# An mLSTM cell followed by a squared-ReLU FFN: k and q pairs a chunk earlier, squares ahead of the numerators' round trip, one marker ahead of a rounding step

## The chip, the cores and the metric

The kernel runs on one core of a Trainium2 chip. The metric is the device time of one execution in microseconds. Three runs of the kernel before took 496.23, 498.50 and 497.52 us; the median is 497.52.

The engines are named as in the profile: PE is TensorE (PEld its weight loads), DVE is VectorE, ACT is ScalarE, POOL is GpSimd, SP is SyncE. DMAs are issued by SP ("SPq") and by POOL, each in the order of its program, and so an issue that waits holds up those behind it.

## What is computed

The first half is an mLSTM cell over 4 batches, 8 heads, 768 steps and a head width of 40:

```
m_new = max(f + m, i);  f_stab = exp(f + m - m_new);  i_stab = exp(i - m_new)
C = f_stab*C + i_stab * outer(v, k);   n = f_stab*n + i_stab*k
y = sigmoid(o) * (C q) / max(|n q|, 1)
```

The second half takes the 3072 rows of 8 x 40 = 320 values as tokens and computes `square(max(x @ w_in, 0)) @ w_out` with w_in of 320 x 2048 and w_out of 2048 x 320.

## The kernel before, in words

**Chunks.** The recurrence is cut into chunks of 128 steps: s = 0 to 23, six to a batch (c = s mod 6 is the place in the batch). Inside a chunk it becomes attention: scores k.q (PE), weights from the gates (ACT), their product (`weighted`, L552, DVE), and matmuls with the values and with the carried state C into the numerators `numT`. Two chunks (256 tokens, a group g) feed one group of the FFN.

**Order.** The order of the program is written out by hand; nothing is scheduled by costs. From chunk 6 on, one loop over `parts` takes n = 0, 1, 2, ...: s = 6 + n // 4 is the chunk, at = n % 4 its quarter, and each part has a quarter of an FFN stage for PE to run beside the attention. From chunk 8 on, even chunks hold the FFN's second product (`ffn2_fast`, L890, a seven-product scheme) and odd chunks the first (`ffn1_open`, `ffn1_close`, L966 and L1015).

**Transposing through DRAM.** k and q are needed with the head width on partitions. `pair_up(s)` copies k and q of chunk s from the inputs to a DRAM tensor `kq_rows`, in pairs of heads, with four DMAs (L308; by SP for s < 10, else by POOL). `load_squares(s)` reads it back as blocks of 32 x 32 with four DMAs on SP (L363) into one of two buffers `kqT` (s mod 2). `turn_kq(s)` transposes the blocks on DVE (L370). Then `scores(s)` can run (L530), and `scale_q` multiplies q by the decays (L600). In even chunk s, quarter 0 has scores(s), turn_kq(s + 1) and weighted(s); scores(s + 1) follow in quarter 1.

**Attention and the marker.** `attend_begin(s)` issues the first half of the numerators' matmuls (L636, L655, L666) and then the marker, a DVE instruction on one element (L628) that reads the result and writes a spare element of an operand of the second half; so the second half (`attend_end`) starts only after the first is through. After that DVE transposes the numerators into `tn` (L686).

**The numerators' round trip.** `store_num` writes tn to DRAM (L701, SP) and `load_num` reads it back with four DMAs (L706), which turns it the rest of the way. `normalise_turned(s)` (L718 to L731, DVE, quarter 2) divides by the denominator and multiplies by the output gate. The rows x make a like round trip: `store_rows` (L757), `load_rows` into xT (L762), `turn_squares` (L769). `load_A` (L394) brings the cumulated decays, which POOL masks (L431) and ACT exponentiates (L461); POOL also forms values times weights (vw, L481) and sums of x for the FFN (L958). Finished tokens go out with L926 and L931 in even chunks.

**Rounding of the weights.** The FFN weights come as pairs of 32-bit words and are put together in 18 pieces: two ACT steps (`words`), three DVE steps (L222, L226, L227) and an addition on POOL (L231). The last piece, two blocks of w_out, is rounded in part n = 4, the first of chunk 7. In part n = 5 the buffers of the rounding are given back (`brought.close()`) and the pool `late` is opened over them; DVE first writes there with L864.

**SP's order in chunk s >= 8, as far as the change touches it:** quarter 1: store_num(s), load_num(s), load_squares(s + 2); then load_A(s + 2) (in even chunks here), the stores of tokens, x rows, the output gate, xT. The squares have to wait for their pairs in `kq_rows`, and for the last reader of their buffer.

Of the kernel before, what the change touches and what calls it, by code (L numbers as in the profile page):

```python
# [14 lines left out]
ALU = mybir.AluOpType  # L15
# [5 lines left out]
def word_as_float(w):  # L21
    return struct.unpack("<f", struct.pack("<I", w))[0]
# [7 lines left out]
def kernel(  # L30
# [27 lines left out]
    nc = tc.nc  # L58
# [33 lines left out]
    brought = ExitStack()  # L92
# [81 lines left out]
    class Rounding:  # L174
# [38 lines left out]
            nc.scalar.activation(low[:, :w], raw[:, :, 0].bitcast(U32), AF.Copy, bias=2.0, scale=2.0 ** -51)  # L213
            self.a.append((mag, low))

        def join(self):
            n = len(self.b)
            dst = pieces[n][0]
            w = dst.shape[1]
            mag, low = (t[:, :w] for t in self.a[n])  # L220
            bits = mag.bitcast(I32)
            nc.vector.tensor_scalar(  # L222
                mag, mag, scalar1=word_as_float(0x38000000), scalar2=word_as_float(0x47EFFFFF),
                op0=ALU.max, op1=ALU.min,
            )
            nc.vector.tensor_scalar(bits, bits, scalar1=3, scalar2=None, op0=ALU.logical_shift_left)  # L226
            nc.vector.scalar_tensor_tensor(  # L227
                bits, in0=self.raws[n][:, :w, 1], scalar=-0x80000000, in1=bits,
                op0=ALU.bitwise_and, op1=ALU.bitwise_xor,
            )  # L230
            nc.gpsimd.tensor_tensor(dst.bitcast(I32), bits, low.bitcast(I32), op=ALU.add)  # L231
            self.b.append(None)
            if n != LENT - 1:
                self.fetch()

        @property
        def done(self):
# [9 lines left out]
    rounding = Rounding()  # L247
# [261 lines left out]
    def scores(s, o=(False, False)):  # L509
        d = st[s]  # L510

        sc = [bank(o[i]) for i in range(2)]
        d["sc"] = sc
        if s >= KQ_SQ:
            if s >= ROT:
                d["sc"] = [t.rearrange("p j t -> p (j t)")[:, : 3 * P].rearrange("p (e t) -> p e t", e=2) for t in sc]
            for e in range(2):
                for late_keys in range(2):
                    for c in range(2):
                        for i in range(2):  # L520
                            rows = slice(DP * i, DP * i + D)
                            start = e == late_keys == 0
                            if s < ROT:
                                j, keys = 2 * late_keys + e, HALVES[c]
                                to, t0 = sc[i][HALVES[c], j, :], 0
                            else:
                                j, keys = 2 * (c ^ late_keys) + e, HALVES[late_keys]
                                to = d["sc"][i][HALVES[c], e, slice(0, DP) if late_keys else slice(DP, 3 * DP)]
                                t0 = DP * late_keys
                            nc.tensor.matmul(  # L530
                                to, lhsT=d["kT"][rows, j, keys], rhs=d["qT"][rows, j, t0:], start=start, stop=True,
                                skip_group_check=True,
                            )
            return
        for j in range(PR):
            for i in range(2):
                rows = slice(DP * i, DP * i + D)
                nc.tensor.matmul(  # L538
                    sc[i][:, j, :], lhsT=d["kT"][rows, j, :], rhs=d["qT"][rows, j, :], start=True, stop=True,
                )  # L540
# [462 lines left out]
    def ffn1_rows(g, q, first):  # L1003
        xT, xs = st["xT", g], st["xs"]
        X, Y, V, Z = st["f1"]
        lo, hi = HALVES
        pairs = (
            ((X, lo, xT[lo, 0, 2, :], False), (Y, hi, xT[hi, 1, 2, :], first)),
            ((V, lo, xT[lo, 1, 2, :], first), (Z, hi, xs[hi, 1, :], False)),
        )  # L1010
        for pair in pairs:
            for n in range(4):
                for cols in HALVES:
                    for to, rows, rhs, start in pair:
                        nc.tensor.matmul(  # L1015
                            to[cols, n, :], lhsT=w_in2[rows, 4 * q + n, cols], rhs=rhs,
                            start=(start and n == 0), stop=True, skip_group_check=True,
                        )
# [35 lines left out]
    def do(f, s):  # L1054
        if 0 <= s < NT:
            f(s)
# [86 lines left out]
    for u in range(8):  # L1143
        s = 2 + u // 2
# [72 lines left out]
    LAST = (17, 17, 17, 17, 18)  # L1217
    assert LAST[-1] == len(pieces)

    for n, (which, g, i) in enumerate(parts):  # L1220
        s, at = 6 + n // 4, n % 4
        if n == 5:
            brought.close()
            late = ctx.enter_context(tc.tile_pool(name="late", bufs=1, side="right"))
        even = s >= 8 and s % 2 == 0
        fast = which == 1
        if at == 0:
            if s < 8 or even:
                do(scores, s)
            if even:  # L1230
                do(turn_kq, s + 1)
            if s < 8 or even:
                do(weighted, s)
        if at == 1:
            do(attend_begin, s)
            if even:
                do(lambda s: scores(s, ("h", "h")), s + 1)
            if fast:
                ffn1_rows(g, 0, True)
            do(attend_end, s)  # L1240
            do(decays, s + 1)
            do(mask, s + 1)
            if n > 4 and not even and not fast:
                do(turn_kq, s + 1)
            do(decay_C, s + 1)
            if s > X_SQ and not fast and not even:
                do(turn_squares, s - 1)
            do(store_num, s)
            do(load_num, s)
            do(load_squares, s + 2)  # L1250
            if even:
                do(load_A, s + 2)
        if 5 <= n < 8:
            sums_of_weights(n - 5)
        if n == 6:
            sums(1, slice(0, NPAIR), (1, 2))
        if n == 8:
            sums_of_weights(3)
            sums(1, slice(0, NPAIR), (3,))
        if n == 9:  # L1260
            sums(1, slice(0, NPAIR), (4,))
        if which == 2 and i == 3 and g == NG - 2:
            sums(g + 1, slice(0, NPAIR), (2,))
        if which == 2 and g > 1 and i < 2:
            sums(g, slice(0, NPAIR), (3 + i,))
        if n == 0:
            ffn1_begin(g)
            sums_of_x(g)
            sums_of_win(2)
        if at == 3 and s >= 8 and s % 2 == 0 and s // 2 - 1 < NG:  # L1270
            sums_of_x(s // 2 - 1)
        if at == 2 and not fast:
            if even:
                do(turn_squares, s - 1)
            if n > 4:
                do(scale_q, s + 1)
        if at == 3:
            if s % 4 == 3:
                for r in range(s + 1, min(s + 5, NT)):
                    half_tanh(r)  # L1280
        if fast:
            if i % 2:
                ffn1_close(g, i // 2, i == 1)
                if at == 1 and g > 2:
                    do(turn_kq, s + 1)
                    do(turn_squares, s - 1)
            else:
                ffn1_open(g, i // 2)
                if i == 0 and g > 2:
                    sums(g - 1, slice(0, NPAIR), (2,))  # L1290
            if at == 2 and g > 2:
                do(scale_q, s + 1)
        elif g == 0:
            ffn2(g, *divmod(i, 2))
        else:
            ffn2_fast(g, i)
        if at == 2:
            do(lambda s: weigh(s, masked=True), s + 1)
            ffn1_square()
            if n < 4:  # L1300
                do(turn_kq, s + 1)
                do(scale_q, s + 1)
            if even:
                do(weighted, s + 1)
            do(normalise_turned, s)
            do(store_rows, s)
            if not even:
                do(load_A, s + 2)
            if s > 6:
                do(load_o, s + 5)  # L1310
            do(load_rows, s)
            if s == 6:
                do(pair_up, s + 3)
        if s > 6 and at == (3 if even else 2):
            do(pair_up, s + 3)
        if s > 6 and at == 3:
            if s == 7:
                load(s + 3)
            do(load, s + 4)
        if n == 3:  # L1320
            turn_halves()
        if n in (9, 25):
            spread_slots(2 + n // 25)
        if at == 0:
            ffn1_square()
        if n < 5:
            while rounding.done < LAST[n]:
                rounding.step()


# [28 lines left out]
```

## Time and profile before

| | us |
|---|---|
| median of three runs | 497.52 |
| the profiled execution | 497.72 |
| its span | 496.0 |
| PE busy | 486.8 |
| PE weight loads busy | 452.8 |
| DVE busy | 346.6 |
| ACT busy | 241.6 |
| POOL busy | 224.6 |

The span is the time from the first instruction of the program to the last; the rest of an execution lies around it. The matmuls' ends are modelled, so that a busy PE can hide short waits; stages that do the same work are therefore compared by their length. Lines such as L370 are lines of the kernel before. In a timeline, a row has its start and its duration in us, the engine, line and operation, what it writes and reads, how many instructions, and in brackets the idle time of the engine before it and who ended that.

### The profile page before, as it was taken

The page shows a single profiled execution, that of the slowest core. Times are in us where ns is not written, and L with a number is a line of the kernel's source. Part 1 is how long each engine was busy: PE and PEld are TensorE (multiplying, and loading weights), DVE is VectorE, ACT ScalarE, POOL GpSimd, SP SyncE. Part 2 cuts the span into 40 slices and gives each one's busy share as a digit, 9 for nine tenths or more (in the row PEclk, how much of TensorE's full clock was granted, in tenths as well). Part 3 has the DMA queues.
Part 4 walks back from the last instruction along what each step waited for, and adds up shares of the span by engine and source line. Part 5 has one row for each costly group of instructions (what it writes and reads, how often), then busy time and mean ns, then how long its engine had stood idle before and what let it go on. Part 6 is the DMA issues. An engine that isn't in the chain of part 4 may idle for free.

```text
span 496.0 us, 15226 instructions
## 1 busy us (share of the span) xinstructions
PE 486.8 (98%) x6169; PEld 452.8 (91%) x6169; DVE 346.6 (70%) x700; ACT 241.6 (49%) x530; POOL 224.6 (45%) x317
## 2 busy tenths in 40 slices
PE   9999989999999999999999999999999999999997
PEld 4877878897799999999999989999999999999997
DVE  8599968978956866866956856766856956735441
ACT  3658878756531560761562850561861560423300
POOL 3256734532589438558547538538544030020000
PEclk9999999999999999999999999999999999999999
DMA  9999996757698678678668768677666532200000
GB/s 189 226 215 213 276 210 143 207 90 138 150 151 187 136 140 177 142 136 178 148 128 177 158 119 170 148 139 166 149 126 142 121 69 80 54 15 15 3 26 28
DMA packets 196167, 68.02 MB, mean 137 GB/s; under 512 B 158704, under 2 KB 186064, under 8 KB 196096
## 3 DMA queue, kind: packets, MB, share of 16 engines
q1 hardware_dynamic: 190560, 57.50, 56.6%
q0 software_dynamic: 5440, 9.34, 8.2%
q8 instruction: 49, 0.80, 0.7%
q14 instruction: 22, 0.18, 0.1%
q10 hardware_dynamic: 96, 0.20, 0.1%
HBM read 54.71 MB, written 18.01 MB: 147 GB/s over the span
## 4 chain that ended last, share of the span: by engine, by line
PE 84%; DVE 10%; DMA 2%; issue 1%; SPq 1%; POOL 0%; DVEq 0%; POOLq 0%
PE h_ps L890 34%; PE h_ps L966 23%; PE h_ps L1015 6%; PE h_ps L799 3%; PE h_ps L836 3%; PE numT L655 2%; PE numT L636 2%; DVE mag L226 2%; PE hp L575 1%; PE idle L1065 1%; PE numT L666 1%; PE tp L538 1%; DMA kqT<-kq_rows 1%; DVE mag L227 1%; PE tp L530 1%
## 5 line engine op out<-in xcount | busy, mean ns | idle before, releaser
L890 PE MATMUL h_ps<-T,S 128*128 128x160 f32 x352 | 51.7, 300 | 0.0
L996 ACT COPY r_sb<-h_ps 128x512 f32<-128x512 f32 x18 | 10.6, 586 | 84.2 <-PE h_ps L966 84.2
L890 PEld LDWEIGHTS h_ps<-T,S 128*128 128x128 f32 x352 | 48.9, 190 | 0.4 <-ACT g_c L1032 0.2
L890 PE MATMUL h_ps<-w_out,g 128*128 128x160 f32 x336 | 49.2, 303 | 0.0
L906 DVE TENSOR_TENSOR y_sb<-y_sb,h_ps 128x160 f32<-128x160 f32 x44 | 14.1, 320 | 47.6 <-PE h_ps L890 47.6
L890 PEld LDWEIGHTS h_ps<-w_out,g 128*128 128x128 f32 x336 | 46.1, 190 | 1.3 <-issue 0.7
L431 POOL TENSOR_SCALAR_AFFINE_SELECT A_bc<-A_bc 64x512 f32<-64x512 f32 x32 | 23.2, 726 | 43.5 <-ACT kq L448 42.2
L966 PE MATMUL h_ps<-xT,w_in 128*128 128x128 f32 x320 | 42.8, 278 | 0.0
L966 PE MATMUL h_ps<-lent_t,w_in 128*128 128x128 f32 x320 | 42.2, 275 | 0.0
L966 PEld LDWEIGHTS h_ps<-xT,w_in 128*128 128x128 f32 x320 | 38.9, 192 | 1.4 <-issue 1.0
L1015 PE MATMUL h_ps<-xT,w_in 64*64 64x128 f32 x960 | 39.1, 272 | 0.0
L966 PEld LDWEIGHTS h_ps<-lent_t,w_in 128*128 128x128 f32 x320 | 38.9, 192 | 0.2 <-issue 0.2
L966 PE MATMUL h_ps<-lent_t 128*128 128x128 f32 x320 | 39.0, 275 | 0.0
L966 PEld LDWEIGHTS h_ps<-lent_t 128*128 128x128 f32 x320 | 37.3, 192 | 0.0
L1015 PEld LDWEIGHTS h_ps<-xT,w_in 64*64 64x64 f32 x960 | 34.8, 133 | 1.3
L461 ACT ACTIVATE A_bc<-A_bc,b_R 128x64 f32<-128x64 f32 (+1 forms) x128 | 35.7, 361 | 0.4
L340 POOL DMA_DIRECT2D va<-in_v_dram x56 | 34.4, 620 | 1.7 <-DMA va<-in_v_dram 0.9
L481 POOL TENSOR_TENSOR vw<-va,A_bc 128x328 f32<-128x328 f32 x13 | 10.2, 788 | 52.3 <-ACT A_bc L461 52.3
L686 DVE STREAM_TRANSPOSE tn<-numT 128x256 f32<-128x256 f32 x36 | 14.0, 429 | 28.4 <-PE numT L636 19.6
L958 POOL TENSOR_TENSOR lent_t<-xT 128x128 f32<-128x128 f32 (+1 forms) x18 | 13.4, 764 | 38.5 <-DVE xT L769 35.5
L799 PE MATMUL h_ps<-xT,w_in 128*128 128x256 f32 x128 | 29.6, 383 | 0.7 <-POOL w_in L231 0.7
L890 PE MATMUL h_ps<-w_out,g_c 128*128 128x160 f32 x192 | 28.0, 302 | 0.0
(200 smaller groups left out, 1189.5 us busy)
## 6 DMA issues: line engine op xcount, KB each, us to landing
A_bc<-a_slots SPq DMA_DIRECT2D x32, 256.0 KB, 4.9
num_rows<-tn SPq DMA_DIRECT2D x18, 256.0 KB, 2.3
kq<-num_rows SPq DMA_DIRECT2D x72, 64.0 KB, 2.0
raw<-in_moe_w_out_dram SPq DMA_DIRECT2D x7, 640.0 KB, 5.3
kqT<-kq_rows SPq DMA_DIRECT2D x34, 128.0 KB, 3.0
og<-in_o_gate_dram SPq DMA_DIRECT2D x24, 160.0 KB, 5.3
out_dram<-y_sb SPq DMA_DIRECT2D x24, 160.0 KB, 3.2
raw<-in_moe_w_in_dram SPq DMA_DIRECT2D x7, 512.0 KB, 5.8
```

The costliest lines, as they stand in the source:

```text
L340: eng.dma_start(dst[HALVES[n], PR * (1 - late_keys) : PR * (2 - late_keys)], src[HALVES[late_keys], PR * m : PR * (m + 1)],)
L431: nc.gpsimd.affine_select(part, part, compare_op=ALU.is_ge, fill=-1e30, base=0, pattern=[[0, PR], [0, 2], [1, DP]], channel_multiplier=-1,)
L461: nc.scalar.activation(A[0][:, x, to], A[0][:, x, to], AF.Exp, bias=b_R[:, b, c, own, x : x + 1],)
L686: nc.vector.transpose(to[:, 2 * m : 2 * m + 2], d["numT"][m].rearrange("p c t -> p (c t)"))
L799: nc.tensor.matmul(hs[i][:, n, :], lhsT=w_in[:, a, fb * P : (fb + 1) * P], rhs=xT[:, :, a, :], start=(n == 0 and a == 0), stop=False,)
L836: nc.tensor.matmul(o_ps, lhsT=st["g2", g][:, fb, j * P : (j + 1) * P], rhs=w_out[:, fb, :], start=(fb == 0), stop=(fb == NF - 1),)
L890: nc.tensor.matmul(to, lhsT=lhsT[:, p], rhs=rhs[:, p, :], start=(start and p == 0), stop=(p == NPAIR - 1), skip_group_check=True,)
L906: add = lambda to, a, b: nc.vector.tensor_tensor(to, a, b, op=ALU.add)
L958: sub = lambda to, a, b: eng.tensor_tensor(to, a, b, op=ALU.subtract)
L966: nc.tensor.matmul(to[:, n, :], lhsT=lhsT[:, 4 * q + n, :], rhs=rhs, start=(start and n == 0), stop=True, skip_group_check=True,)
L996: nc.scalar.copy(m1[:], X[:])
L1015: nc.tensor.matmul(to[cols, n, :], lhsT=w_in2[rows, 4 * q + n, cols], rhs=rhs, start=(start and n == 0), stop=True, skip_group_check=True,)
```

## The change

Three things move; no arithmetic and no DMA is added or removed.

1. `pair_up` runs one chunk earlier: in chunk s it now takes s + 4 instead of s + 3. Chunk 7 does both 10 and 11.
2. From chunk 8 on, `load_squares` no longer follows `load_num`. Even chunk s issues the squares of s + 2 in quarter 0, ahead of its store_num, and those of s + 3 at the end of quarter 3, after the token store L931 and ahead of store_num of chunk s + 1. Odd chunks issue none.
3. The last rounding step's DVE work is split: the first two instructions (L222, L226) stay in part n = 4, the third (L227) comes after the marker of chunk 7, in part n = 5, followed by POOL's addition. The pool `late` is opened after that instead of at the start of the part.

```diff
-        def join(self):
+        def join(self, till=None):
...
-            nc.vector.tensor_scalar(
-                mag, mag, scalar1=word_as_float(0x38000000), scalar2=word_as_float(0x47EFFFFF),
-                op0=ALU.max, op1=ALU.min,
-            )
-            nc.vector.tensor_scalar(bits, bits, scalar1=3, scalar2=None, op0=ALU.logical_shift_left)
+            if till == 1:
+                self.join_to(mag, bits)
+                return
+            if till is None:
+                self.join_to(mag, bits)
             nc.vector.scalar_tensor_tensor(
                 bits, in0=self.raws[n][:, :w, 1], scalar=-0x80000000, in1=bits,
                 op0=ALU.bitwise_and, op1=ALU.bitwise_xor,
...
+        def join_to(self, mag, bits):
+            nc.vector.tensor_scalar(
+                mag, mag, scalar1=word_as_float(0x38000000), scalar2=word_as_float(0x47EFFFFF),
+                op0=ALU.max, op1=ALU.min,
+            )
+            nc.vector.tensor_scalar(bits, bits, scalar1=3, scalar2=None, op0=ALU.logical_shift_left)
...
-        if n == 5:
-            brought.close()
-            late = ctx.enter_context(tc.tile_pool(name="late", bufs=1, side="right"))
...
             if s < 8 or even:
                 do(weighted, s)
+            if even:
+                do(load_squares, s + 2)
         if at == 1:
             do(attend_begin, s)
+            if n == 5:
+                rounding.join(2)
...
             do(store_num, s)
             do(load_num, s)
-            do(load_squares, s + 2)
+            if s < 8:
+                do(load_squares, s + 2)
             if even:
                 do(load_A, s + 2)
+        if n == 5:
+            brought.close()
+            late = ctx.enter_context(tc.tile_pool(name="late", bufs=1, side="right"))
...
         if s > 6 and at == (3 if even else 2):
-            do(pair_up, s + 3)
+            if s == 7:
+                pair_up(s + 3)
+            do(pair_up, s + 4)
...
+        if even and at == 3:
+            do(load_squares, s + 3)
...
         if n < 5:
-            while rounding.done < LAST[n]:
+            while rounding.done < LAST[n] - (n == 4):
                 rounding.step()
+            if n == 4:
+                while len(rounding.a) < LAST[n]:
+                    rounding.words()
+                rounding.join(1)
```

## The prediction, made before the result was known

> **What bounds the kernel now.** I read the page first: TensorE is busy nearly throughout, and the chain that ended last runs mostly over it.
>
> ```profile
> PE 486.8 (98%) x6169; PEld 452.8 (91%) x6169; DVE 346.6 (70%) x700; ACT 241.6 (49%) x530; POOL 224.6 (45%) x317
> PE 84%; DVE 10%; DMA 2%; issue 1%; SPq 1%; POOL 0%; DVEq 0%; POOLq 0%
> ```
>
> The change adds and removes no arithmetic, so it can only win or lose gaps of TensorE after about 120 us. To find these I went through the chain in order of time and compared equal stages. From the first L890 block of an even chunk to its second block (step 0 of the FFN product, then the attention) takes 6.95 us in chunks 8, 10, 14 and 22, but 8.74 us in chunk 16 (282.44 to 291.18). Chunks 12 and 18 start a batch and have fewer matmuls: 6.57 and 7.12 us. Odd chunks repeat to 0.02 us (29.82 us, or 29.36 where the batch ends). So what this part of the kernel loses is 1.79 us in chunk 16, 0.55 in chunk 18, about 0.2 each in 12 and 20. The waits of VectorE tell why in two lines:
>
> ```profile
> DVE dm L718 <- DMA kq<-num_rows: 4.2, 5, 1.0
> DVE kqT L370 <- DMA kqT<-kq_rows: 3.6, 2, 2.0
> ```
>
> The second is the wait for the "squares" (the blocks of k and q) in chunks 16 and 18; the first, for the numerators' round trip, is short and comes five times. VectorE and TensorE of chunk 16 in the timeline (start, duration, idle before it):
>
> ```profile
> 286.58 1.25 DVE L370 STREAM_TRANSPOSE kqT<-kqT 128x1024 f32<-128x1024 f32 x1 [2.00 <-DMA kqT<-kq_rows]
> 287.75 0.98 DVE L552 TENSOR_TENSOR A_bc<-tp,A_bc 128x384 f32<-128x384 f32 x2
> 288.66 1.20 DVE L885 TENSOR_TENSOR g_c<-g_c 128x1024 f32<-128x1024 f32 x1
> 289.78 0.31 DVE L906 TENSOR_TENSOR y_sb<-h_ps,y_sb 128x160 f32<-128x160 f32 x1
> 290.12 0.16 DVE L628 TENSOR_SCALAR kq<-numT 1x1 f32<-1x1 f32 x1
> 288.32 0.33 PE L636 MATMUL numT<-kq,C 40*64 40x128 f32 x3 [0.73 <-DVE A_bc L552]
> ```
>
> The late transpose delays L552, for which TensorE waits, and then the marker L628, for which it waits again. The DMA queue of SyncE in chunks 16 to 17, and VectorE's answer in 17:
>
> ```profile
> 307.80 3.04 SPq L762 DMA_DIRECT2D xT<-x_rows  x4
> 310.95 0.40 SPq L931 DMA_DIRECT2D out_dram<-y_sb  x1
> 311.45 0.38 SPq L701 DMA_DIRECT2D num_rows<-tn  x1
> 313.86 1.74 SPq L706 DMA_DIRECT2D kq<-num_rows  x4
> 315.71 2.72 SPq L363 DMA_DIRECT2D kqT<-kq_rows  x4
> ...
> 317.09 0.23 DVE L718 TENSOR_SCALAR dm<-kq 128x8 f32<-128x8 f32 x1 [0.70 <-DMA kq<-num_rows]
> ```
>
> The reader is to see the order: squares wait behind a round trip of 4 us, and the numerators' store itself goes out as soon as L931 is through. Last, chunk 7:
>
> ```profile
> 120.13 0.82 DVE L227 SCALAR_TENSOR_TENSOR mag<-raw,mag 128x640 int32<-128x640 int32 x1
> 120.19 0.39 PE L666 MATMUL numT<-vw,kq 64*64 64x41 f32 x16
> 120.98 0.16 DVE L628 TENSOR_SCALAR kq<-numT 1x1 f32<-1x1 f32 x1
> 121.19 0.44 PE L666 MATMUL numT<-vw,kq 64*64 64x41 f32 x16 [0.61 <-DVE kq L628]
> ```
>
> The marker needs only the first L666 (over at 120.58) but stands behind L227.
>
> **What the Trainium skill says.** "Perfetto Trace Analysis", Identifying the Most-Contended Engine, takes LDWEIGHTS busy and not matmul busy as the measure of TensorE; at 91% here there is little left to win, as the stage lengths say too. "DMA: Bandwidth & Descriptors", Anatomy of one DMA, says that DMA engines don't wait on semaphores: the wait is on the issuing sequencer before dispatch. The trace agrees: L706 begins at 313.86, when the store of 311.45 has landed, and L363 comes after. The same section puts the fixed cost of a DMA at about 2.0 us; here the numerators' store lands in 2.0 to 4.1 us (median 2.3). Issuing engines are not separate DMA queues, same page, says that what POOL and SyncE issue shares 16 engines, so moving pairs on POOL's queue saves no transfer.
>
> **Part 1, the squares' wait goes.** Squares of an even chunk s+2 are now issued in chunk s ahead of its numerators, those of an odd chunk s+3 at the end of even chunk s: most of a chunk before L370 wants them. Their pairs are written a chunk earlier still, so they don't wait for those. Both L370 waits go: 1.79 + 0.55 = 2.34 us of TensorE. Should a new wait stand there, this is 0; more than 2.7, with chunks 12 and 20, isn't there.
>
> **Part 2, the marker.** It can start at 120.65 in place of 120.98 (in chunk 8 it starts 0.07 after L666's end): 0.33 us. L227 then fills VectorE's idle 1.23 us before the transposes at 122.36. POOL's last rounding step, L231 (121.03 to 122.57), starts at about the same time; its readers are TensorE's seventh L836, near 125.6, and L864 at 124.95. Closing the pool later changes no order. Without that cover L231 costs at most its own 1.54 us.
>
> **Part 3, POOL.** Same issues in all, but chunk 7 has two pairs: one more set is 1.10 + 1.02 = 2.1 us. Behind it stand the loads of chunks 10 and 11 (0.95 us of a wait there absorbs part), the mask at 142.96, spread_slots, vw at 148.25 and the sums L958 to 152.47. The exponentials L461 (145.94) become up to 0.6 us late, while their reader L552 comes at 152.38, 4.2 us after their end; the sums end by 154.6 at most and TensorE reads them from 155.00. I take 0; at most 1 us once.
>
> **Part 4, the numerators' store waits on SyncE.** One set of squares costs 2.33 to 3.69 us of SyncE; I take 2.5, the sets with idle DMA engines. In even chunks it stands between xT (L762) and the store: in 12, xT ends at 215.69, so the store goes at about 218.3 instead of 216.78; in 18 at 330.4 instead of 328.59. The rows are then in 1.5 to 1.8 us later, and L718 there (226.01 and 337.83) begins over 2 us after they are in now. Cost 0. The copies of A, issued behind, go 0.5 to 2.5 us earlier, since no squares follow L706.
>
> In odd chunks 9 to 21 the squares stand between L931 and the store, and SyncE has no slack: the store follows L931's end by 0.1 to 0.4 us (1.3 in chunk 21). New start of L718: L931's end + 0.1 + 2.5 + 0.1 + 2.2 (landing) + 1.75 (L706) + 1.8 (last landing) = +8.45 us. When is that too late? From L718 to L552 VectorE needs 5.4 us (206.15 to 211.55), from L552 to the marker's end 2.53 (chunk 16 above); TensorE wants the marker 6.27 us after the even chunk's first L890 (chunk 10), 6.1 where a batch starts. So L718 must begin 1.7 us before that L890, or 1.9. L931's ends are 162.20, 198.14, 236.00, 272.40, 311.35, 347.37, 382.36, so L718 comes at 170.65, 206.6, 244.45, 280.85, 319.8, 355.8, 390.8; wanted by 171.3, 207.4, 244.0, 280.8, 318.7, 355.8, 392.8. Late: 0.45 in chunk 13, 0.05 in 15, 1.1 in 17, others in time: 1.6 us. Against it, earlier copies of A should let the x rows of even chunks land sooner (now 2.7 to 5.2 us), and with them xT and L931; 0.5 us would leave 0.6. Scatter of landings adds some. I take 1.0; ends 0 and 12 (below).
>
> **Sum.** -2.34 - 0.33 + 0 + 1.0 = -1.7 us. The profiled execution took 497.72 us with a span of 496.0 (1.72 around it), so 496.0 with a span of 494.3. Its time is 0.2 above the median of the three runs, 497.52; there it is 495.8.
>
> **Rivals.** (a) Full gain: no odd round trip is late, perhaps the 0.2 of chunks 12 and 20 go too: -2.67 to -3.1, 494.4 to 494.9. For: quiet DMA engines after 200 us (12% busy at 202 to 204), so squares would pass quickly there. Against: margins of 0 to 0.8 us.
> (b) Another wait takes the place: L718 late by what L370 was; gain and loss cancel, 497.3. For: chunks 15 and 17 already wait 1.03 and 0.70 for the numerators.
> (c) Slower, by SyncE's head of line in odd chunks. If squares cost 3.4 us there (as in chunk 9) and landings are slow (4.1 and 3.9 in chunks 11 and 15), L718 is 2 us later than reckoned: late by 1.3, 1.2, 2.45, 2.05, 3.1, 2.0 and 0, about 12 us, so 506.9. Half of it, 1 us later, costs 6.0: 500.9. Above 500.0, half a per cent, it needs some 0.85 us more than reckoned.
> (d) That the change doesn't do what it says is excluded: the built order shows squares ahead of the store and the marker ahead of L227.
>
> **Chances.** Forecast 0.42 (own range 494.9 to 497.0), (a) 0.26, (b) 0.12, (c) 0.20. About 0.5% (2.5 us) is what a measurement of this kernel can tell from no change. Faster by that (under 495.0) is (a) and the forecast's edge: 0.30. Slower is (c): 0.20. Rest 0.50. The range leaves out less than a tenth below (more than the full gain) and the worse half of (c) above: 494.0 to 501.0.
>
> **What would show it.** Right: no L370 wait for kqT; 6.95 us between the L890 blocks in chunk 16; marker of chunk 7 next to the first L666; squares directly ahead of L701 in SyncE's order. Waits of L718 in odd chunks grow from 4.2 us to some 10, TensorE losing about 1 of it. Wrong: L636 or L666 waiting for VectorE in chunks 10 to 22 (then (c)), or TensorE's L966 near 155 us waiting for POOL's sums.

## The result, and the profile after

The changed kernel takes 515.17 us (median of 4 executions, 510.71 to 517.43); the kernel before, beside it, 496.88. The ratio is 1.036, 95% interval 1.027 to 1.045: **slower by 3.6%**, where I had forecast 495.8 us and a range up to 501.0. All ratios leave out executions more than 1.5% above the fastest of the same kernel, so for a kernel whose own times scatter by more (the four small loads below: 13 of 20 are left out) the ratio is nearer to one than the medians of all its runs, and both are given.

The profiled execution took 516.86 us with a span of 515.1 (before: 497.72 and 496.0). In the code after, the lines of the chunks that the prediction names have moved down by 7 (those of the last rounding step, L227 and L231, keep their numbers): the normalise L718 is L725, the squares L363 are L370, their transpose L370 is L377, the numerators' store L701 is L708. Busy times, granted clock in 40 slices and the chain that ended last:

```profile
PE 498.0 (97%) x6169; PEld 461.9 (90%) x6169; DVE 344.5 (67%) x700; ACT 241.9 (47%) x530; POOL 222.9 (43%) x317
...
PEclk9999979999999969999989999999999999999999
...
PE 75%; DVE 13%; DMA 7%; issue 2%; SPq 1%; DVEq 0%
```

The clock row of the kernel before:

```profile
PEclk9999999999999999999999999999999999999999
```

The engines run as many instructions as before, but DMA and VectorE have gone from 12% of the chain to 20%, and three slices of the clock row are below full. The waits, VectorE's first, then TensorE's (total us, times, longest):

```profile
DVE dm L725 <- DMA kq<-num_rows: 28.8, 10, 6.7
DVE kqT L377 <- DMA kqT<-kq_rows: 0.5, 1, 0.5
```

```profile
PE numT L643 <- DVE A_bc L559: 8.3, 3, 4.5
```

The squares' wait is nearly gone (3.6 to 0.5 us), as planned. In its place the numerators' wait has gone from 4.2 to 28.8 us, and TensorE waits for VectorE behind it.

**Where the time went.** From the end of one chunk's last attention matmul to the next chunk's (a chunk's stage, from here on), in the two traces: chunk 6 ends 2.96 us later in the changed kernel (half clock from 64.5 to 71.3 us, in code that the change doesn't touch); chunk 7 is 0.33 shorter; chunks 8 to 23 are 16.5 longer in sum; the tail is the same. Of the 16.5: chunk 10 +7.0, 14 +4.5, 20 +2.2, 11 +2.0, 18 +1.2, the small ones (9, 12, 22) +1.0, and chunk 16 -1.5. Chunk 11 apart, to which I come below, it is even chunks that are longer, each behind an odd chunk that waited. (Chunk 16 is no gain of the move: with the squares at their old place, experiment 1, it is just as short. The other chunks are 18.0 longer together, and against experiment 1 chunks 8 to 23 are 18.5 longer.) Chunk 9 into 10, the worst, in the timeline of the changed kernel: SyncE's queue first, then VectorE and TensorE (start, us, what, idle before it):

```profile
164.50 1.86 SPq L769 DMA_DIRECT2D xT<-x_rows  x4
166.48 0.40 SPq L938 DMA_DIRECT2D out_dram<-y_sb  x1
167.34 2.28 SPq L370 DMA_DIRECT2D kqT<-kq_rows  x4
169.72 2.02 SPq L708 DMA_DIRECT2D num_rows<-tn  x1
174.31 1.73 SPq L713 DMA_DIRECT2D kq<-num_rows  x4
...
179.58 0.17 DVE L725 TENSOR_SCALAR dm<-kq 128x8 f32<-128x8 f32 x1 [6.71 <-DMA kq<-num_rows]
...
183.83 1.23 DVE L377 STREAM_TRANSPOSE kqT<-kqT 128x1024 f32<-128x1024 f32 x1
184.99 0.98 DVE L559 TENSOR_TENSOR A_bc<-tp,A_bc 128x384 f32<-128x384 f32 x2
...
185.56 0.49 PE L643 MATMUL numT<-kq,C 40*64 40x128 f32 x3 [4.51 <-DVE A_bc L559]
```

The same part of the kernel before, with no squares between the token store and the numerators:

```profile
162.31 0.37 SPq L701 DMA_DIRECT2D num_rows<-tn  x1
164.38 1.75 SPq L706 DMA_DIRECT2D kq<-num_rows  x4
...
169.33 0.17 DVE L718 TENSOR_SCALAR dm<-kq 128x8 f32<-128x8 f32 x1
```

There the tile was ready at 162.17. In the changed kernel the numerators' tile was ready at 165.27. Its store went out at 169.72, behind the token store and the squares; issuing it took 2.02 us, and it landed at 174.29, 4.58 after its issue began. The loads' last byte came at 179.46. VectorE stood 6.71 us at L725 with the rest of the odd chunk and the transpose for the even one queued behind it, so L559 came at 184.99, and TensorE had been out of work for 4.51 us.

That is not all of it. The clock in three stretches right after (start:end, length, busy us of PE, PEld, DVE, ACT, POOL with counts, clock, DMA share, GB/s):

```profile
183.98:190.10 6.12, 4.54 (x111) 4.21 (x111) 3.51 (x6) 4.76 (x8) 1.33 (x2) 0.50 1.04 158
190.10:194.22 4.12, 4.12 (x16) 4.12 (x17) 2.19 (x5) 0.00 (x0) 1.30 (x1) 0.50 0.43 91
265.90:269.30 3.40, 3.40 (x97) 3.40 (x96) 1.77 (x4) 3.02 (x6) 0.90 (x2) 0.50 1.18 145
```

After the two gaps of over 2 us (4.51 in chunk 10, 2.51 in chunk 14) TensorE ran at half its clock, for 10.2 and 3.4 us. Chunk 11 is longer by 2.04 us with no new wait of TensorE: it is half of the 4.12 us in the second line. The Trainium skill ("TensorE: Matmul & The Clock Gate", Part 1, What's actually happening) says that an idle window of about 3.4 us halves the clock and that the window runs free. The lengths of the stretches here, 3.41 us, twice and three times that, agree with such a window; but a gap of 2.51 us was followed by half clock as well, and in other runs shorter ones were (last section). With 2.04 in chunk 11, 1.24 in chunk 10 (marker to end of the attention 2.54 us, 1.30 before) and 0.91 in chunk 14 (2.21 against 1.30), the clock cost at least 4.2 of the 16.5 us.

The two small claims can be read off as well. Chunk 16's transpose has no wait any more, and from its first L897 block to the second (299.57 to 306.86) it takes 7.29 us where it took 8.74 (I had said 6.95; with the squares at their old place, experiment 1, it is 7.14); chunk 7's marker stands ahead of L227:

```profile
302.26 1.24 DVE L377 STREAM_TRANSPOSE kqT<-kqT 128x1024 f32<-128x1024 f32 x1
...
305.80 0.16 DVE L635 TENSOR_SCALAR kq<-numT 1x1 f32<-1x1 f32 x1
```

```profile
123.62 0.16 DVE L635 TENSOR_SCALAR kq<-numT 1x1 f32<-1x1 f32 x1 [1.34 <-PE numT L673]
123.80 0.82 DVE L227 SCALAR_TENSOR_TENSOR mag<-raw,mag 128x640 int32<-128x640 int32 x1
```

### The profile page after: what moved, and what is told of

It is laid out like the page before. It is cut to its first block, busy times and chain, and to the rows that moved or that the text cites. A ratio compares the mean times of both kernels' runs of the same rounds, so it can differ in the third digit from the quotient of the medians.

```text
span 515.1 us, 15219 instructions
## 1 busy us (share of the span) xinstructions
PE 498.0 (97%) x6169; PEld 461.9 (90%) x6169; DVE 344.5 (67%) x700; ACT 241.9 (47%) x530; POOL 222.9 (43%) x317
## 4 chain that ended last, share of the span: by engine, by line
PE 75%; DVE 13%; DMA 7%; issue 2%; SPq 1%; DVEq 0%
PE h_ps L897 28%; PE h_ps L973 19%; PE h_ps L1022 5%; DMA num_rows<-tn 3%; PE h_ps L843 3%; PE h_ps L806 3%; DMA kq<-num_rows 3%; PE numT L662 2%; PE numT L643 2%; PE numT L673 1%; PE hp L582 1%; PE idle L1072 1%; DVE mag L241 1%; PE tp L545 1%; SPq L713 1%
## 5 line engine op out<-in xcount | busy, mean ns | idle before, releaser
L897 PE MATMUL h_ps<-T,S 128*128 128x160 f32 x352 | 51.7, 300 | 0.0
L897 PEld LDWEIGHTS h_ps<-T,S 128*128 128x128 f32 x352 | 48.9, 190 | 0.4 <-ACT g_c L1039 0.2
L897 PE MATMUL h_ps<-w_out,g 128*128 128x160 f32 x336 | 49.2, 303 | 0.0
L913 DVE TENSOR_TENSOR y_sb<-y_sb,h_ps 128x160 f32<-128x160 f32 x44 | 14.1, 320 | 50.3 <-PE h_ps L897 50.3
L897 PEld LDWEIGHTS h_ps<-w_out,g 128*128 128x128 f32 x336 | 46.1, 190 | 1.3 <-issue 0.9
L438 POOL TENSOR_SCALAR_AFFINE_SELECT A_bc<-A_bc 64x512 f32<-64x512 f32 x32 | 21.9, 686 | 57.6 <-ACT kq L455 56.3
L693 DVE STREAM_TRANSPOSE tn<-numT 128x256 f32<-128x256 f32 x36 | 14.0, 428 | 28.2 <-PE numT L643 19.3
L488 POOL TENSOR_TENSOR vw<-va,A_bc 128x328 f32<-128x328 f32 x13 | 11.4, 875 | 49.2 <-ACT A_bc L468 49.1
L806 PE MATMUL h_ps<-xT,w_in 128*128 128x256 f32 x128 | 31.8, 404 | 0.7 <-POOL w_in L231 0.7
L897 PE MATMUL h_ps<-w_out,g_c 128*128 128x160 f32 x192 | 30.1, 316 | 0.0
```

What stands on the lines that cost most here:

```text
L438: nc.gpsimd.affine_select(part, part, compare_op=ALU.is_ge, fill=-1e30, base=0, pattern=[[0, PR], [0, 2], [1, DP]], channel_multiplier=-1,)
L488: nc.gpsimd.tensor_tensor(d["vw"][:].rearrange("p (own x) d -> p own x d", own=2), d["va"][:].rearrange("p (own x) d -> p own x d", own=2) ...
L693: nc.vector.transpose(to[:, 2 * m : 2 * m + 2], d["numT"][m].rearrange("p c t -> p (c t)"))
L806: nc.tensor.matmul(hs[i][:, n, :], lhsT=w_in[:, a, fb * P : (fb + 1) * P], rhs=xT[:, :, a, :], start=(n == 0 and a == 0), stop=False,)
L897: nc.tensor.matmul(to, lhsT=lhsT[:, p], rhs=rhs[:, p, :], start=(start and p == 0), stop=(p == NPAIR - 1), skip_group_check=True,)
L913: add = lambda to, a, b: nc.vector.tensor_tensor(to, a, b, op=ALU.add)
```

## The experiments

Theory A: the loss is made by SyncE's order. What stands ahead of the odd chunks' numerators on that queue delays their store, VectorE waits at the normalise, TensorE runs dry, and its clock drops. The rivals: POOL's extra pairs or the split rounding step (B), chunk 8's long issuing alone (C), squares early at any place (D), and the squares' data in the DMA engines, whoever issues them (E). Diffs are against the changed kernel unless said otherwise.

**1. The squares back at their old place.**

```diff
-            if even:
-                do(load_squares, s + 2)
...
             do(load_num, s)
-            if s < 8:
-                do(load_squares, s + 2)
+            do(load_squares, s + 2)
...
-        if even and at == 3:
-            do(load_squares, s + 3)
```

> The changed kernel with the squares put back behind the numerators' load, where they stood before; the earlier pairs and the split rounding step of chunk 7 stay. Theory A (the place of the squares on SyncE makes all of the loss): 495.5 to 497.5 us, the waits at the normalise (L718 before, about 4 us in sum) as before, chunk 7's stage at 16.2 us, and the wait of the transposed squares in chunks 16 and 18 back at about 3.6 us unless the earlier pairs remove it. Rival B (POOL's extra pairs or the split rounding step make the loss): 505 us or more, with the loss already in chunk 7 or 8.

Measured: 495.74 us (before 497.23), ratio 0.999, interval 0.996 to 1.002. Chunk 7's stage is 16.17 us, the waits at the normalise 3.8 us. So the earlier pairs and the split rounding step cost nothing that can be measured: B falls, and the whole loss lies in the squares' place.

**2 and 3. Only the even chunks' squares moved; only the odd chunks'.**

Even only:

```diff
-            if s < 8:
+            if s < 8 or not even:
                 do(load_squares, s + 2)
...
-        if even and at == 3:
-            do(load_squares, s + 3)
```

Odd only:

```diff
-            if even:
-                do(load_squares, s + 2)
...
-            if s < 8:
+            if s < 8 or even:
                 do(load_squares, s + 2)
```

> The changed kernel with only the even chunks' squares moved (to their quarter 0); the odd chunks load theirs behind the numerators as before. Theory A, that the odd chunks' squares make most of the loss: 497 to 501 us; chunk 8 keeps its wait of about 2.6 us at the normalise, chunks 9, 13, 17 and 19 fall from 4 to 7 us to under 1.5. Rival C, that chunk 8's 6.4 us of issuing starts a delay that the later chunks hand on: 507 to 513 us, with chunk 9 still waiting 4 us or more and a long stage in chunk 10.

> The changed kernel with only the odd chunks' squares moved (to the end of the even chunk before); the even chunks load theirs behind the numerators as before. Theory A, that the odd chunks' squares make most of the loss: 505 to 513 us, waits of 3 to 6 us at the normalise in chunks 9, 13, 17, 19 and stages of 21 to 25 us in the even chunks after them. Rival C (chunk 8 starts it): 496 to 500 us, those waits under 2 us.

Measured: even only 498.81 us, ratio 1.002 (0.999 to 1.005); odd only 515.82 us, ratio 1.036 (1.029 to 1.044), above my range of 505 to 513. The profiled execution of odd only took 525.35 us, so its waits may be on the high side. The waits of VectorE at the normalise, even only:

```profile
DVE dm L725 <- DMA kq<-num_rows: 7.8, 6, 2.6
```

and odd only:

```profile
DVE dm L725 <- DMA kq<-num_rows: 34.0, 8, 8.1
```

The odd chunks' squares make the loss by themselves; C falls. Chunk 8 does keep its 2.6 us wait in the first of the two (its squares' issuing took 5.81 us), and it comes to nothing at the end that can be told: the even chunks do have slack, though not the 2 us or more that I had given each. In the odd-only kernel even the profiled chunk 9, without a late chunk 8 ahead of it, waits 8.1 us.

**4. The odd chunks' squares a quarter sooner,** in the even chunk's quarter 2, just ahead of its x rows, even squares at the old place. I meant this as the better version. Against "odd only":

```diff
+            if even:
+                do(load_squares, s + 3)
             do(store_rows, s)
...
-        if even and at == 3:
-            do(load_squares, s + 3)
```

> The odd chunks' squares moved one quarter further forward, into quarter 2 of the even chunk before, between its token store and its x rows; the even chunks load theirs behind the numerators as before. Theory A (what costs is only that squares stand directly ahead of the numerators' store): 493.5 to 496 us, the waits at the normalise about 4 us in sum, that of the transposed squares under 1 us. Rival D (issuing squares at any place ahead of the numerators delays something, the x rows first): 499 to 508 us, and a wait at the x rows or the copies of A in place of that at the normalise.

Measured: 511.67 us, ratio 1.030 (1.022 to 1.038). This is outside my expectation and above rival D's range too (499 to 508); rival D's waits are there (the loads of the transposed x rows make VectorE wait 9.2 us). SyncE's queue of that kernel from chunk 8 to chunk 9:

```profile
156.50 4.47 SPq L370 DMA_DIRECT2D kqT<-kq_rows  x4
161.08 2.76 SPq L764 DMA_DIRECT2D x_rows<-x_sb  x1
...
166.18 2.76 SPq L769 DMA_DIRECT2D xT<-x_rows  x4
169.06 0.40 SPq L938 DMA_DIRECT2D out_dram<-y_sb  x1
169.56 0.38 SPq L708 DMA_DIRECT2D num_rows<-tn  x1
```

The squares are a quarter away from the numerators, and yet the store goes out at 169.56 with its tile ready at 163.20. The x rows are stored late, so their loads back are late, so the token store and the numerators behind them on the same queue are late. Theory A as I had put it ("directly ahead of the numerators") was too narrow: anything that SyncE does from the x rows on reaches the odd numerators. What is left open here is whether time on SyncE or the data does it.

**5. The squares issued from ScalarE's queue.**

```diff
-                nc.sync.dma_start(
+                (nc.sync if s < 10 else nc.scalar).dma_start(
```

> The changed kernel, its squares at their new places, but from chunk 10's on issued from ScalarE's queue and not from SyncE's. Theory A (the loss is SyncE's order: the numerators' store and loads stand behind the squares' issuing): the odd chunks' store is issued within 1.5 us of the end of its tile again, the waits at the normalise fall to 4 to 8 us in sum, 494 to 499 us; the issuing, 2.5 to 4 us a chunk, goes to ScalarE, which is busy for 47%. Rival E (the squares' data in the DMA engines ahead of the numerators makes them late, whoever issues them): the store is issued early but lands 4 us or more after its issue, the waits stay at 15 us or more in sum, 506 to 515 us.

Measured: 531.83 us, ratio 1.065 (1.058 to 1.073), far outside both expectations. The two waits that tell why, VectorE's at the normalise:

```profile
DVE dm L725 <- DMA kq<-num_rows: 6.4, 6, 2.0
```

and ScalarE's:

```profile
ACT y_sb L917 <- DMA kqT<-kq_rows: 49.9, 6, 10.1
```

What A said of the numerators holds: with the same squares at the same point of the program but off SyncE, their wait falls from 28.8 to 6.4 us in sum, and the odd store is issued 0.4 us after its tile on average, where the changed kernel has 3.3. The time is lost elsewhere. In chunk 10 the four issues span 9.14 us, of which the issuing itself takes 1.3; in the rest ScalarE's queue waits between them. Each of the waiting loads waits for the very semaphore that is to report its own landing, and in the trace these waits end when an earlier DMA of SyncE on the same semaphore lands: the store of the x rows at 181.83, a load of A at 184.83, the load of the output gate at 185.82. The same three end most of this waiting in chunks 12 to 18. The copy L917 stands behind these issues (the line above names the squares because their issues come last before it), with VectorE's L913 behind L917 (28.2 us of waits) and the attention's marker behind that. So one queue's head of line was traded for a worse one, and this run doesn't show what the change would be worth without it.

**6 and 9. Issue time without data.** Squares at the old place, and at the end of each even chunk eight loads of 64 bytes that nothing reads (four, with `range(4)`, in the second kernel). Against experiment 1:

```diff
+    tiny = consts.tile([8, 16], F32)
...
+        if even and at == 3:
+            for m in range(8):
+                nc.sync.dma_start(tiny[m : m + 1, :], k[0, 0, m : m + 1, :16])
```

> The squares behind the numerators' load as before, the earlier pairs and split rounding step kept, and at the end of each even chunk from chunk 8 on eight loads of 64 bytes each on SyncE, which nothing reads: some 3 us of issuing with no data to speak of, where the changed kernel has the odd chunks' squares. Theory A (SyncE's issue time): waits at the normalise of 2 to 5 us in chunks 9, 13, 15, 17, 19, 504 to 514 us. Rival E (the squares' data): 495.5 to 500 us, waits under 8 us in sum.

> As with the eight small loads ahead of the odd chunks' numerators, but four of them, 1.3 us of issuing in place of 2.6. Theory A with no slack in the odd chunks (each us of SyncE time there is a us of the end, times the eight odd chunks and what the clock adds): half of the loss of the eight, 502 to 505 us. Theory A with slack (the first us or so is free, as the forecast had it for half of the lateness): 496.5 to 500 us.

Measured: eight, 511.26 us against 497.28 beside it, ratio 1.028 (1.023 to 1.032). Four, 503.73 us against 496.77 (medians of all executions; the profiled one took 506.08), ratio 1.0055 (1.0015 to 1.0095). SyncE's queue with eight, chunk 9:

```profile
167.04 0.36 SPq L938 DMA_DIRECT2D out_dram<-y_sb  x1
167.46 2.62 SPq L1334 DMA_DIRECT2D tiny<-in_k_dram  x8
170.18 0.36 SPq L708 DMA_DIRECT2D num_rows<-tn  x1
172.22 1.75 SPq L713 DMA_DIRECT2D kq<-num_rows  x4
```

This decides for A against E as the main cause: 512 bytes move no data to speak of, and 2.62 us of SyncE at this place, in each of eight even chunks (2.35 to 3.15 us in the others, short waits included), cost 14.0 us of the end. Of the waits that I expected in five chunks, those in 9, 13 and 17 came (4.1, 4.1 and 5.3 us); 15 and 19 had 0.2 and 1.2. Half as many loads cost 7.0 us by the medians and 2.7 by the ratio: they cost something, but whether half as much as the eight is not settled, and so neither is how much of the first microsecond is free. The changed kernel loses some 4 us more than the eight (in chunks 8 to 23 of the profiles, against experiment 1: 18.5 us, and 11.9 with the eight). Its squares take 0.3 us longer to issue (2.96 on average), and its odd chunks' store and last load land 0.3 and 0.4 us later than before the change, which the data may well do; a run with data alone would be needed to show it.

**7. The odd squares between the numerators' store and its loads,** where SyncE waits for the store to land. Against experiment 1:

```diff
             do(store_num, s)
+            if s >= 8 and not even:
+                do(load_squares, s + 2)
             do(load_num, s)
-            do(load_squares, s + 2)
+            if s < 8 or even:
+                do(load_squares, s + 2)
```

> The odd chunks' squares between the numerators' store and its load, where SyncE otherwise waits some 1.7 to 2 us for the store to land; all else as with the squares at their old place. Theory A: the load's issue is late by the squares' 2.5 to 3.5 us less the 1.8 us of that wait, so 0.7 to 1.7 us, the waits at the normalise 6 to 14 us in sum, 496 to 500 us. Rival E (data): the squares' packets are ahead of the numerators' loads, which land 2 us or more later than with the squares behind them: 500 to 507 us.

Measured: 502.34 us, ratio 1.010 (1.005 to 1.016); waits at the normalise 13.6 us in sum, and no wait for the squares. The waits are as A had them, at their upper end; the time is above its range and inside E's. In chunk 9 the squares took 3.40 us to issue and the loads began 3.59 us after the store's issue had ended (1.70 in the kernel before). The last load's landing, on the other hand, is 1.86 us after its issue on average in the odd chunks 9 to 21, and 1.86 in the kernel before: the squares' data ahead of them didn't hold them up. So it is issue time here as well, by this one profile, at a price that I had put too low.

**8. The kernel before, profiled again.**

> The kernel before, unchanged, profiled once more. If the wait of DVE's transpose of the squares in chunks 16 and 18 (3.6 us in the profile, of which the forecast took 2.34 us off the end) belongs to the kernel, it is there again at 2.5 to 4.5 us and chunk 16's stage is again 20.2 to 20.7 us. If it was that one execution's late landing, it is under 1 us or in another chunk, and chunk 16's stage is 18.6 to 19.2 us as with the squares at their old place.

```profile
DVE dm L718 <- DMA kq<-num_rows: 3.3, 4, 1.8
DVE kqT L370 <- DMA kqT<-kq_rows: 1.2, 1, 1.2
```

The squares' wait is 1.2 us once, in chunk 12, none in 16 or 18; chunk 16's stage is 18.85 us where the first profile had 20.45, chunk 18's 18.22 where it had 18.83. Chunks 8 to 23 are 1.25 us shorter and chunk 7 is 0.33 shorter. This execution took 497.72 us like the first all the same, because chunk 6 ended 1.49 us later in it, with 3.41 us at half clock. So the two waits on which the forecast's gain rested belonged to that one execution; the wait belongs to the kernel, but it moves and is often about a microsecond (1.3 once in experiment 1, too).

**10. The odd squares in the x rows' gap,** between the store of the x rows and their loads back. Against experiment 1:

```diff
             do(load_num, s)
-            do(load_squares, s + 2)
+            if s < 8 or even:
+                do(load_squares, s + 2)
...
                 do(load_o, s + 5)
+            if even:
+                do(load_squares, s + 3)
             do(load_rows, s)
```

> The odd chunks' squares in the even chunk before, between the store of the x rows and their loads back, where SyncE otherwise sits for some 2.5 us until the x rows have landed; the even chunks' squares at their old place, earlier pairs and split rounding step kept. Theory A (what counts is by how much SyncE reaches the odd chunks' numerators later): the 2.5 us of issuing fit the gap but for up to 1 us, so the numerators' store is late by 0 to 1 us, waits at the normalise 4 to 9 us in sum, 495.5 to 501 us. Rival D (squares at any place of the even chunk cost what they cost at its end): 506 to 515 us.

Measured: 506.47 us, ratio 1.017 (1.011 to 1.023), waits at the normalise 18.6 us: above A's range and at the lower edge of D's.

```profile
155.37 8.25 SPq L370 DMA_DIRECT2D kqT<-kq_rows  x4
164.07 1.87 SPq L769 DMA_DIRECT2D xT<-x_rows  x4
166.05 0.40 SPq L938 DMA_DIRECT2D out_dram<-y_sb  x1
166.55 1.10 SPq L708 DMA_DIRECT2D num_rows<-tn  x1
```

The gap was there, but the four loads don't take 2.5 us in it: 8.25 us in chunk 8, 5.2 to 7.3 in chunks 10 to 18, 3.2 in chunk 20. When the first of them was issued in chunk 8, ten DMAs had been issued and had not landed (by the landings that the trace has): two loads of A, a token store, the store of the x rows, the output gate and five of POOL's. In chunk 20, where the set took 3.2 us, there were two. The pauses between the four are 0.21 us in sum, so that SyncE was issuing and not waiting for semaphores. Issuing was slow where much was in flight; why, no run here shows.

**11. The token store behind the odd numerators,** squares at the old place. Against experiment 1:

```diff
-            nc.sync.dma_start(out[t * P : (t + 1) * P, :], y0[:])
+            st["held"] = (out[t * P : (t + 1) * P, :], y0)
...
             do(load_num, s)
+            if "held" in st:
+                to, y = st.pop("held")
+                nc.sync.dma_start(to, y[:])
             do(load_squares, s + 2)
...
+    if "held" in st:
+        to, y = st.pop("held")
+        nc.sync.dma_start(to, y[:])
```

> The squares at their old place, earlier pairs and split rounding step kept, and the even chunks' last token store put behind the odd chunks' numerators instead of ahead of them. Theory A: the odd chunks' store is issued within 0.1 us of the end of its tile, 0.2 to 1.4 us sooner in chunks 9, 13, 15, 17 and 19, the waits at the normalise (3.8 us in sum with the store ahead) fall under 2 us, 493.5 to 496 us. Rival F (in the undisturbed kernel those waits are covered, so nothing is won): 495 to 497.5 us, not to be told from the kernel with the squares at their old place.

Measured: ratio 1.001 (0.998 to 1.004), medians 499.71 and 496.77. No gain, as rival F had it or a little worse. In the profiled execution (507.45 us) the wait moved on, to what now stands behind the token store:

```profile
DVE kqT L377 <- DMA kqT<-kq_rows: 9.4, 4, 3.2
DVE dm L725 <- DMA kq<-num_rows: 4.8, 6, 1.2
```

The squares, which now stand behind the token store too, make VectorE wait. Numerators and squares are both close to being late in this order of the queue.

**All runs together.** Mean time from the end of the numerators' tile to the normalise in the odd chunks 9 to 21 of each profile, VectorE's waits there in sum over the kernel, and the median time of all executions:

| kernel | tile to normalise, us | waits, us | time, us |
|---|---|---|---|
| before, two profiles | 7.57, 7.51 | 4.2, 3.3 | 496.8 to 497.3 |
| squares at old place | 7.56 | 3.8 | 495.7 |
| even only | 7.58 | 7.8 | 498.8 |
| token store behind | 7.66 | 4.8 | 499.7 |
| four small loads | 8.76 | 11.5 | 503.7 |
| between store and loads | 9.04 | 13.6 | 502.3 |
| eight small loads | 9.60 | 20.1 | 511.3 |
| x rows' gap | 10.58 | 18.6 | 506.5 |
| changed kernel | 10.79 | 28.8 | 515.2 |
| quarter 2 | 11.07 | 18.1 | 511.7 |
| odd only | 11.97 | 34.0 | 515.8 |

Up to about 7.6 us the round trip costs nothing that can be measured; beyond it, each microsecond on this mean goes with 3 to 7 us of the end (2 for the four small loads, if their ratio is taken). The squares from ScalarE (7.57, 6.4, 531.8) are the exception, by their other wait, and so in part is the token store behind the numerators, by its wait for squares. No version beats the kernel before by more than can be measured.

## Why the prediction was wrong

**The step that failed is Part 4, the numerators' store on SyncE, in its odd chunks: +1.0 us taken, 18.0 us measured in chunks 8 to 23 (16.5 in sum, with chunk 16 shorter by 1.5).** Its mechanism, order and place were right, and rival (c) was this mechanism; it had a chance of 0.20 and a price, 12 us, that comes near what the stalls cost without the clock (18.0 less at least 4.2, so 13.8 at most).

The sum in it was "L931's end + 8.45 us". Measured from the same line's end to L725 in chunks 9 to 21: 12.71, 9.64, 11.63, 10.09, 9.88, 10.72, 10.23 us, 10.7 on average. Term by term, means over these seven: squares' issuing 2.96 where I took 2.5; the store from issue to landing 3.16 where I took 2.2 (six of these seven landings are in the trace before, with a mean of 2.9: even there the odd chunks were slower than the median); the last load's landing 2.27 where I took 1.8; the loads' issuing 1.95 for 1.75, because once, in chunk 13, it took 3.27. Each is small, and all went one way. I had taken values of idle engines and medians over all chunks. With the means of the odd chunks alone from the trace before (2.79, 2.87, 1.86 and 1.87, in the same order) the sum would have been 9.6: about half of what was missing could be read before the change, and the other 1.1 us came with it. Margins of 0 to 0.8 us could not bear a sum that is short by 2.2.

The relief from earlier x rows (0.5 us taken) is 0.28 us on average: L931's end stood 0.37 us after the tile's end before, and 0.09 after. In chunk 9 it went the other way (0.04 to 1.60), behind the late chunk 8.

**"Even chunks cost 0"** was right on the end to what can be told (experiment 2), but not by its working: squares took up to 6.4 us there, not 2.5, and chunk 8's normalise waited 2.6 us.

**The clock** was not in the sum at all, and this is the second step that failed. A stall of TensorE was priced at its own length; stalls of 4.51 and 2.51 us were followed by 13.7 us at half clock, worth at least 4.2 us.

**Part 1,** the squares' wait: it went, as said (3.6 to 0.5 us), and chunk 16's stage is 1.46 us shorter. But 2.34 us was one execution's value: the second profile of the kernel before has 1.2 us of this wait in all, worth 0.96 us in chunk 12, and its chunk 16 is as short without the move. A microsecond is less than the runs can tell from nothing.

**Part 2,** the marker: 0.33 us expected, 0.33 measured (stage of chunk 7, 16.50 to 16.17). The second profile of the kernel before has 16.17 as well, so that this, too, was a wait that only comes at times: that the numbers agree is luck and no sign that the split did it.

**Part 3,** POOL's pairs: 0 expected; nothing measured (experiment 1).

**What would show it** was put rightly for the wrong case: the sign named for rival (c), L643 (L636 before) waiting for VectorE, is there with 8.3 us. The waits at the normalise, forecast at some 10 us, came to 28.8.

## What to carry to other kernels

Look at a DMA queue as an engine with its own in-order program: before a transfer is moved forward, find the transfer behind it with the least slack, and charge it the issue time, with the values seen when the queue is loaded. Here 2.6 us of issuing without data, ahead of a round trip with next to no slack and at eight places, cost 14 us. A margin of less than the scatter of its terms is no margin, and a wait to be removed should be seen in a second profile before it is counted as gain.

## What the runs showed of the hardware that I had not expected

- The price of issuing varies. The same four loads of the squares took SyncE 2.3 us at best and 8.25 at worst, single ones 0.30 to 3.42 us. The dearest sets were issued with many DMAs under way (ten at the 8.25 us of experiment 10, 14 at the 6.38 of chunk 8 in the changed kernel, three at its 2.28 of chunk 9); no run separates this from other causes.
- Issuing as such can be the whole cost. The Trainium skill ("DMA: Bandwidth & Descriptors", Issuing engines are not separate DMA queues) says that starting DMAs from several engines saves only the sequencer's time, "usually small relative to the DMA itself"; eight loads of 64 bytes, 2.62 us of SyncE, in each of eight even chunks were worth 14.0 us of the kernel here.
- Moving issues to another engine's queue is no cure by itself: ScalarE stood still for up to 10.1 us, most of it because the squares that it was to issue waited for semaphores that DMAs of SyncE were still using (experiment 5).
- Half clock came in stretches of 3.41, 6.83 and 10.24 us. In chunks 8 to 23 of all these traces each idle gap of TensorE of 2.0 us or more (2.04 to 5.55) went with one. Of the gaps of 1.3 to 2.0 us five did (1.36, 1.41, 1.66, 1.90 and 1.99) and seven did not (1.33 to 1.94), so that length alone doesn't decide there. The traces of experiments 1 and 2 have no gap over 0.9 us in these chunks and no half clock.
